# A lag of two FFN steps for w_out, in place of hand-balanced VectorE slots, in a long convolution with a maxout FFN

## The chip, the cores and the metric

The kernel runs on one core of a Trainium2 chip. The metric is the device time of one execution in microseconds (us), as the median of the runs. Engines are called PE (TensorE), DVE (VectorE), ACT (ScalarE), POOL (GpSimd) and SP (SyncE, which here only issues DMAs).

## The reference

A long convolution per channel by FFT, gated by its own input, feeds a feed-forward layer with the maximum of three products. Shapes: B = 4, S = 12544, D = 128, filter order 64, d_ff = 768; everything is float32.

```python
h_filt = (np.maximum(pos_emb @ w1, 0.0) @ w2) * np.exp(-0.01 * np.arange(S))[:, None]
u = x * v
L = 2 * S
y = np.fft.irfft(np.fft.rfft(u, n=L, axis=1) * np.fft.rfft(h_filt, n=L, axis=0)[None],
                 n=L, axis=1)[:, :S, :]
t = (x * y).reshape(B * S, D)
h = np.maximum(np.maximum(t @ moe_w1, t @ moe_w2), t @ moe_w3)
out = h @ moe_w_out
```

## The kernel before

The Fourier transforms are matmuls, done in four steps over a 128 x 98 factoring of the sequence. The filter's transform and the convolution of batch 0 come first (up to about 330 us). Then the FFN of batch b runs on PE while the convolution of batch b+1 is woven into it, for b = 0, 1, 2 (330 to about 1931 us). The FFN of the last batch runs alone at the end, in another form, with its own step order. The order of instructions on every engine is the program's order: the kernel switches the scheduler off, and each engine takes its instructions one after the other.

**FFN.** A batch has 32 tiles of 392 tokens, and a tile six steps `f`, each for 128 of the 768 hidden columns. A step is called a slot here; a batch has 192. The three-way maximum is computed as lin + max(max(a, 0), b), where a and b are products with differences of the weights and `lin` is a product folded into the output. `up` (from L689) multiplies with the first difference into `pa`, takes relu on ACT into `hid` (L694), multiplies with the second into `pb` and takes the maximum on DVE in place (L697). `down` (from L700) accumulates hid with a block of w_out into `ops`, in a tile's first step also gt with `lin`. After a tile's last step ACT copies `ops` to `ot` (L710) and POOL issues its store (L712). `pa` and `pb` rotate through three PSUM banks of the pool `hps`, `hid` through three buffers, `ops` has one bank. In slot f = 3 `t_last` makes the next tile's input: inverse-transform matmuls into `yps` and a product with x on DVE (`gt`, L684). Sums and differences of the two loaded halves (`t_sums`, `even` and `zt`) stand ahead of slot f = 1: on POOL in batch 0 and in the first half of later ones (L662, L663), on DVE in the second half (L666).

**The loop.** In each slot comes: `up` of this step, `down` of the step before it (`late`), `t_last` where due, and then the convolution's steps for this slot, from a list that `conv_steps` writes ahead.

**Convolution.** Its first part handles 32 blocks of channels (`u_` functions) and takes slots 0 to about 55 or 62. After it, 45 pairs of frequencies follow each other, spread evenly, with two or three slots between starts. Pair x starts at slot s:

- s: `g_quarter` does both matmul stages into a double bank `psq` of the pool `cps` (two such banks, shared with `yps` and the first part): the forward one of pair x and the inverse one of pair x - 3
- s+1: `g_fold` copies half of psq to `eo` on ACT (L484) and forms sum and difference on DVE into `cb` (L487, two operations of 128 x 512); half is the spectrum of pair x, half the result of x - 3, stored later by POOL (L495)
- s+2, s+3: `q_swap` exchanges real and imaginary parts on ACT into `xs` (L502 and L503 for each half of the partitions, 32 x 512 each)
- then `q_re` (L506) and `q_im` (L511) multiply with the filter's spectrum on DVE, POOL adds (L514), and `q_unfold` (L518) forms a difference and a sum of 128 x 256 on DVE for the inverse stage of three pairs later.

The planner in `conv_steps` keeps an estimate of DVE work per slot, `load`, and puts each product and each of the two unfold operations in the slot with least of it among those allowed:

```python
a = emptiest(range(s + 4, min(s + 5, last - 2) + 1), 0.7)
at(a, 0, q_re, g)
a = emptiest(range(a, min(s + 6, last - 1) + 1), 0.7)
at(a, 0, q_im, g)
for q in range(2):
    at(emptiest(range(a + 1, last + 1), 0.55), 0, q_unfold, g, q)
```

Of the kernel before, what the change touches and what calls it, by code (L numbers as in the profile page):

```python
# [9 lines left out]
FP32 = mybir.dt.float32  # L10
I32 = mybir.dt.int32
U16 = mybir.dt.uint16
ALU = mybir.AluOpType
ACTF = mybir.ActivationFunctionType
PSUM = bass.MemoryType.PSUM
P = 128
# [11 lines left out]
LATE = 3  # L28
# [61 lines left out]
def kernel(  # L90
# [15 lines left out]
    nc = tc.nc  # L106
    NG, _, _, B, NB = x.shape
    FO, S = posT.shape
    D = w2.shape[1]
    DFF = moe_w1.shape[1]  # L110
    NF = DFF // P
    NK = N1 // 2
# [37 lines left out]
    def halves_mm(out, lhsT, rhs, start, stop):  # L150


        for h in range(2):
            nc.tensor.matmul(out[64 * h:64 * h + 64], lhsT[:, 64 * h:64 * h + 64], rhs,  # L154
                             start=start, stop=stop, skip_group_check=True)
# [181 lines left out]
    us, uts, ws, hts, eos, xts, xss, abs_, pss, sqs, zss = ({} for _ in range(11))  # L337
# [157 lines left out]
        nc.gpsimd.dma_start(  # L495
            zd[b][2 * z:2 * z + 2].rearrange("k c t a f -> (k c t) a f"), zss.pop(z))

    def q_swap(g, at):
        if at == 0:
            xss[g] = cvp.tile([P, 2, 2, D], FP32, tag="xs", name="xs", bufs=3)  # L500
        xt, xs = xts[g], xss[g]
        nc.scalar.mul(xs[at:at + 32], xt[at + 32:at + 64], -1.0)  # L502
        nc.scalar.copy(xs[at + 32:at + 64], xt[at:at + 32])  # L503

    def q_re(g):
        nc.vector.tensor_tensor(out=xts[g], in0=xts[g],  # L506
# [6 lines left out]
                                op=ALU.mult)  # L513
        nc.gpsimd.tensor_tensor(out=xts[g], in0=xts[g], in1=xs[:], op=ALU.add)  # L514

    def q_unfold(g, q):
        y, ab = xts[g], xss[g]
        nc.vector.tensor_tensor(out=ab[:, q], in0=y[:, 0], in1=y[:, 1],  # L518
                                op=(ALU.subtract, ALU.add)[q])
        if q:  # L520
            abs_[g] = xss.pop(g)

    def g_second(g):
        ps = state["cv"][1].tile([P, 512], FP32, tag="cv", name="ps2")
# [47 lines left out]
    def conv_steps(b, done):  # L572


        out = []

        def at(slot, late, fn, *args):
            out.append((slot, late, len(out), fn, args))

        per_pair = 170 / (NK + LATE + 0.6 * (NU - done))
        for u in range(done, NU):
            s = (u - done) * 0.6 * per_pair + 9
            at(max(0, int(s) - 9), 0, u_load, b, u)
            at(int(s) - 6, 0, u_mul, u)
            at(int(s) - 5, 0, u_planes, u)
            at(int(s) - 4, 0, u_dma, u)
            at(int(s), 0, u_join, u)
            at(int(s + 1), 1, u_first, u)  # L590
        s0 = int((NU - done - 1) * 0.6 * per_pair + 9) + 6
        load = [(1.2 if i % NF == 3 else 0.6) + (1.4 if i % NF == 1 and b > 1 and i >= NT * NF // 2 else 0)
                for i in range(NT * NF)]
        for x in range(NK + LATE):
            load[s0 + int(x * per_pair) + 1] += 1.4

        def emptiest(among, cost):
            s = min(among, key=lambda i: load[i])
            load[s] += cost
            return s  # L600

        for x in range(NK + LATE):
            s = s0 + int(x * per_pair)
            g, z = x if x < NK else None, x - LATE if x >= LATE else None
            at(s, 1, g_quarter, g, z)
            at(s + 1, 0, g_fold, g, z)
            at(s - 4, 0, w_load, x)
            if z is not None:
                at(s + 3, 0, g_store, b, z)
            if g is None:  # L610
                continue
            if g % 2 == 0:
                at(s - 4, 0, q_load, g, min(2, NK - g))
                at(s - 1, 0, h_load, g, min(2, NK - g))
            at(s + 2, 0, q_swap, g, 0)
            at(s + 3, 0, q_swap, g, 64)
            last = s0 + int((x + LATE) * per_pair) - 1
            a = emptiest(range(s + 4, min(s + 5, last - 2) + 1), 0.7)
            at(a, 0, q_re, g)
            a = emptiest(range(a, min(s + 6, last - 1) + 1), 0.7)  # L620
            at(a, 0, q_im, g)
            for q in range(2):
                at(emptiest(range(a + 1, last + 1), 0.55), 0, q_unfold, g, q)
        slots = {}
        for s, _, _, fn, args in sorted(out, key=lambda r: r[:3]):
            slots.setdefault(s, []).append((fn, args))
        return slots
# [3 lines left out]
    NT = P // 4  # L631
    zts, xTs, gs, pos_, obs = ({} for _ in range(5))

    def t_load(b, i):
        zt = hp.tile([N1, 2, 512], FP32, tag="zt", name="zt", bufs=2)
        for c in range(2):
            if b == 0:
                nc.sync.dma_start(
                    zt[NK * c:NK * c + NK],
                    zd[b].rearrange("(g a) c t f -> g a c t f", a=2)[  # L640
                        :, :, c, 2 * i:2 * i + 2, :].rearrange("g a t f -> g a (t f)"))
                continue
            q, j = divmod(i, NT // 2)
            for a in range(2):
                nc.sync.dma_start(
                    zt[NK * c:NK * c + NK, a].rearrange("g (t f) -> g t f", t=2),
                    zd[b].rearrange("(g a) c t q f -> g a c t q f", a=2)[
                        :, a, c ^ (a & q), 2 * j:2 * j + 2, q, :])
        zts[b, i] = zt[:, 0], zt[:, 1]
        if i % 2:  # L650
            return
        xT = hp.tile([D, 2, 4, NB], FP32, tag="xT", name="xT", bufs=2)
        for c in range(GC):
            nc.sync.dma_start(xT[c * NG:(c + 1) * NG].rearrange("d i p n -> d (i p) n"),
                              x[:, 4 * i:4 * i + 8, c, b, :])
        xTs[b, i], xTs[b, i + 1] = xT[:, 0], xT[:, 1]

    def t_sums(i, eng=nc.gpsimd):
        z0, z1 = zts[i]
        even = hp.tile([N1, 512], FP32, tag="even", name="even", bufs=2)  # L660
        if i[0] == 0 or i[1] < NT // 2:
            eng.tensor_tensor(out=even[:], in0=z0, in1=z1, op=ALU.add)  # L662
            eng.tensor_tensor(out=z1, in0=z0, in1=z1, op=ALU.subtract)  # L663
        else:
            for out, op in ((even[:], ALU.add), (z1, ALU.subtract)):
                nc.vector.scalar_tensor_tensor(out=out, in0=z1, scalar=sign_t[:, 0:1], in1=z0,  # L666
                                               op0=ALU.mult, op1=op)
        zts[i] = even[:], z1
# [31 lines left out]
    def down(i, f, h):  # L700
        if f == 0:
            pos_[i] = ops.tile([D, 512], FP32, tag="ops", name="ops")
            halves_mm(pos_[i][:, 0:N], lin[:], gs[i][:].rearrange("d p n -> d (p n)"), True,
                      False)
        halves_mm(pos_[i][:, 0:N], wo_sb[:, f, :], h[:], False, f == NF - 1)
        if f < NF - 1:
            return
        gs.pop(i)
        o = op_.tile([D, 4, NB], FP32, tag="o", name="ot")
        nc.scalar.copy(o[:].rearrange("d p n -> d (p n)"), pos_.pop(i)[:, 0:N])  # L710
        dst = outT.rearrange("d (p b n) -> d p b n", b=B, n=NB)[:, 4 * i[1]:4 * i[1] + 4, i[0], :]
        nc.gpsimd.dma_start(dst, o[:])  # L712
# [160 lines left out]
    for u in range(0, NU, 2):  # L873
        t = uts.pop(u)
        for v in range(2):
            if u + 4 < NU:
                u_mul(u + 4 + v)
            at = 4 * (u + v)
# [11 lines left out]
    for i in (1, 2):  # L890
        nc.vector.tensor_tensor(out=w_sb[i][:], in0=w_sb[i][:], in1=w_sb[0][:],
                                op=ALU.subtract)
# [3 lines left out]
    cvp = pro.enter_context(tc.tile_pool(name="cvp0", bufs=3))  # L896
# [123 lines left out]
    cvp = conv.enter_context(tc.tile_pool(name="cvp", bufs=3))  # L1020
# [5 lines left out]

    tiles = [(b, i) for b in range(B) for i in range(NT)]
    LAST = (B - 1) * NT
    late = None
    for n, (b, i) in enumerate(tiles[:LAST]):  # L1030
        if i == 0:
            beside = {}
            beside = conv_steps(b + 1, EARLY if b == 0 else 0)
        if n == 0:
            t_load(*tiles[0])
            t_load(*tiles[1])
            t_sums(tiles[0], nc.vector)
            t_last(tiles[0])
        for f in range(NF):

            if i < NT - 2:
                if f == 0:
                    t_load(*tiles[n + 2])
            elif i == NT - 1 and f < 2 and n + 1 + f < len(tiles):
                t_load(*tiles[n + 1 + f])
            turn_ = i == NT - 1
            if f == (3 if turn_ else 1):
                t_sums(tiles[n + 1], nc.vector if turn_ else nc.gpsimd)
            if f == 4 and n + 1 == LAST:
                t_sums(tiles[n + 2], nc.vector)  # L1050
            h = up((b, i), f)
            if late is not None:
                down(*late)
            late = ((b, i), f, h)
            if f == (4 if turn_ else 3):
                t_last(tiles[n + 1])
            if f == 5 and n + 1 == LAST:
                t_last(tiles[n + 2])
            s = i * NF + f
            run(beside.pop(s, ()))  # L1060
            if s == NT * NF - 1:
                assert not beside, sorted(beside)
    first = up((B - 1, 0), 0)
    down(*late)
    conv.close()


# [20 lines left out]
    step, b = 0, B - 1  # L1088
    for i in range(0, NT, 2):
        h = {}  # L1090
# [63 lines left out]
```

## Time and profile before

| | |
|---|---|
| median of 3 runs | 2353.33 us (2351.71 to 2353.9) |
| profiled execution | 2353.33 us, its span 2351.5 us |
| mean granted PE clock | 0.995 |
| PE busy 330 to 842, 842 to 1387, 1387 to 1931 us | 509.2, 536.7, 533.7 us |
| DVE busy in the same | 340.6, 377.4, 379.3 us |
| ACT busy in the same | 273.8, 288.1, 286.9 us |
| relu, L694 | 768 of 499 ns |
| maximum, L697 | 768 of 558 ns |
| exchange, L502 and L503 | 270 of 628 ns, 270 of 616 ns |
| fold, L487 (128 x 512) | 252 of 683 ns |
| products, L506 and L511 | 135 of 689 ns, 135 of 738 ns |
| unfold, L518 | 270 of 468 ns |

The durations are means of one profiled execution and include whatever slowed an instruction down while it ran; the timeline shows each one by itself. A wait in the profile is the idle time of an engine before an instruction, put down to what released it last.

### The profile page before, as it was taken

To read this page: it belongs to the slowest core of one execution; us is meant where nothing else is said; L and a number is where in the kernel's file an instruction comes from. 1 tells how busy PE (TensorE), PEld (TensorE's weight loads), DVE (VectorE), ACT (ScalarE), POOL (GpSimd) and SP (SyncE) were. 2 spreads that over 40 slices of the span, in tenths; PEclk is the share of its full clock that TensorE was granted. 3 is DMA by queue.
4 is the path that set the end of the run, shared out by engine and by line. 5 is a ranking of instruction groups with operands and counts; after the bars stand their busy time and mean duration, and the time that the engine had idled before them with its cause. 6 is when DMAs were issued, how large, how long until landed. Compare 5 with 4: busy or idle time off the path is not lost.

```text
span 2351.5 us, 67998 instructions
## 1 busy us (share of the span) xinstructions
PE 2300.1 (98%) x27853; PEld 1373.9 (58%) x27853; DVE 1528.8 (65%) x2798; ACT 1172.7 (50%) x2124; POOL 976.0 (42%) x1153
## 2 busy tenths in 40 slices
PE   8999989999999999999999999999999999999998
PEld 7889866655545546654454446655454546666665
DVE  5668857756777747757787747757777755444443
ACT  2678844456665624446666624446666632222222
POOL 1045424334444434434333324434333326666666
PEclk9999999999999999999999999999999999999999
DMA  7869969979898869969899849969899922222221
GB/s 163 195 192 267 292 154 187 165 173 230 225 240 218 206 126 190 187 144 239 226 236 240 221 114 190 187 139 241 229 231 242 229 81 70 56 54 66 68 54 22
DMA packets 473145, 410.92 MB, mean 175 GB/s; under 512 B 328004, under 2 KB 374231, under 8 KB 472834
## 3 DMA queue, kind: packets, MB, share of 16 engines
q1 hardware_dynamic: 433504, 317.61, 60.9%
q0 software_dynamic: 26400, 75.72, 11.1%
q10 hardware_dynamic: 12930, 13.25, 1.8%
q8 instruction: 219, 3.59, 0.7%
q14 instruction: 92, 0.75, 0.1%
HBM read 262.77 MB, written 84.67 MB: 148 GB/s over the span
## 4 chain that ended last, share of the span: by engine, by line
PE 87%; DMA 5%; DVE 2%; issue 2%; ACT 2%; SPq 0%; POOL 0%; ACTq 0%; POOLq 0%; DVEq 0%
PE pa L154 20%; PE pb L154 19%; PE ops L154 16%; PE ops L757 6%; PE ps L408 5%; PE yps L154 5%; PE psq L462 3%; PE ps L163 3%; PE ps L154 3%; PE psq L472 2%; PE gps L926 1%; PE sps L944 1%; DMA zt<-zd 1%; DMA wt<-wq_const 1%; PE pm L323 1%
## 5 line engine op out<-in xcount | busy, mean ns | idle before, releaser
L694 ACT ACTIVATE hid<-pa 128x392 f32<-128x392 f32 x768 | 383.4, 499 | 683.0 <-PE pa L154 657.3
L697 DVE TENSOR_TENSOR hid<-hid,pb 128x392 f32<-128x392 f32 x768 | 428.7, 558 | 425.6 <-PE pb L154 332.5
L154 PE MATMUL pa<-gt,w_sb 128*64 128x392 f32 x3072 | 648.3, 499 | 0.8 <-DVE gt L684 0.8
L154 PE MATMUL pb<-gt,w_sb 128*64 128x392 f32 x3072 | 638.9, 493 | 3.6 <-ACT hid L694 3.6
L154 PE MATMUL ops<-hid,wo_sb 128*64 128x392 f32 x2304 | 478.9, 493 | 15.6 <-DVE hid L697 15.6
L154 PEld LDWEIGHTS pb<-gt,w_sb 128*64 128x64 f32 x3072 | 223.3, 137 | 288.2 <-issue 271.0
L514 POOL TENSOR_TENSOR cb<-cb,xs 128x512 f32<-128x512 f32 x135 | 174.9, 1296 | 444.5 <-DVE xs L511 155.0
L154 PEld LDWEIGHTS ops<-hid,wo_sb 128*64 128x64 f32 x2304 | 165.7, 137 | 232.6 <-issue 168.4
L154 PEld LDWEIGHTS pa<-gt,w_sb 128*64 128x64 f32 x3072 | 196.1, 137 | 137.8 <-issue 93.2
L712 POOL DMA_DIRECT2D out_dram<-ot x96 | 74.6, 777 | 422.4 <-ACT ot L710 285.8
L502 ACT ACTIVATE xs<-cb 32x512 f32<-32x512 f32 x270 | 169.5, 628 | 111.5 <-DVE cb L487 107.3
L487 DVE TENSOR_TENSOR cb<-psq,eo 128x512 f32<-128x512 f32 (+1 forms) x288 | 175.1, 649 | 72.5 <-ACT eo L484 72.5
L419 DVE TENSOR_TENSOR spec<-ps,high 128x360 f32<-128x360 f32 (+1 forms) x204 | 142.0, 738 | 114.3 <-ACT high L417 113.8
L503 ACT COPY xs<-cb 32x512 f32<-32x512 f32 x270 | 166.3, 616 | 3.1
L417 ACT COPY high<-ps 128x360 f32<-128x360 f32 (+1 forms) x102 | 77.3, 762 | 170.2 <-PE ps L408 112.7
L408 PEld LDWEIGHTS ps<-f1q,uT 98*64 98x64 f32 x3072 | 132.2, 137 | 34.6 <-issue 32.4
L154 PEld LDWEIGHTS yps<-f4p,even 90*64 90x64 f32 x2048 | 116.3, 138 | 41.0 <-issue 36.4
L408 PE MATMUL ps<-f1q,uT 98*64 98x90 f32 x3072 | 136.6, 241 | 3.1 <-DVE spec L419 2.6
L684 DVE TENSOR_TENSOR gt<-yps,xT 128x392 f32<-128x392 f32 x128 | 72.5, 567 | 97.7 <-PE yps L154 55.6
L154 PE MATMUL yps<-f4p,even 90*64 90x49 f32 x2048 | 125.6, 221 | 3.3 <-DMA f4p<-f4p_const 3.3
L154 PE MATMUL yps<-f4p,zt 90*64 90x49 f32 x2048 | 127.4, 223 | 0.0
L518 DVE TENSOR_TENSOR xs<-cb 128x256 f32<-128x256 f32 x270 | 115.9, 468 | 3.6 <-POOL cb L514 3.1
(130 smaller groups left out, 3343.0 us busy)
## 6 DMA issues: line engine op xcount, KB each, us to landing
ht<-hd SPq DMA_DIRECT2D x264, 256.0 KB, 5.9
wt<-wq_const SPq DMA_DIRECT2D x144, 256.0 KB, 6.7
zd<-cb POOLq DMA_DIRECT2D x135, 256.0 KB, 6.1
zt<-zd SPq DMA_DIRECT2D x384, 90.0 KB, 3.2
sq<-spec SPq DMA_DIRECT2D x264, 128.0 KB, 7.2
ut<-in_xr_dram SPq DMA_DIRECT2D x128, 196.0 KB, 4.1
ut<-in_vr_dram SPq DMA_DIRECT2D x128, 196.0 KB, 4.3
xT<-in_x_dram SPq DMA_DIRECT2D x256, 98.0 KB, 4.0
```

The costliest lines, as they stand in the source:

```text
L154: nc.tensor.matmul(out[64 * h:64 * h + 64], lhsT[:, 64 * h:64 * h + 64], rhs, start=start, stop=stop, skip_group_check=True)
L408: nc.tensor.matmul(ps[64 * c:64 * c + 64, 256 * i + h * N1:256 * i + (h + 1) * N1], t[:, 2 * ((at + i) % 8) + h].rearrange("n r t -> n (r ...
L417: nc.scalar.copy(high, v[:, 0])
L419: nc.vector.tensor_tensor(out=spec[:, :, a, at:at + n], in0=v[:, 1], in1=high, op=op)
L487: nc.vector.tensor_tensor(out=cb[:, a, lo:hi], in0=ps[:, lo:hi], in1=eo[:, lo:hi], op=op)
L502: nc.scalar.mul(xs[at:at + 32], xt[at + 32:at + 64], -1.0)
L503: nc.scalar.copy(xs[at + 32:at + 64], xt[at:at + 32])
L514: nc.gpsimd.tensor_tensor(out=xts[g], in0=xts[g], in1=xs[:], op=ALU.add)
L518: nc.vector.tensor_tensor(out=ab[:, q], in0=y[:, 0], in1=y[:, 1], op=(ALU.subtract, ALU.add)[q])
L694: nc.scalar.activation(h[:], pa[:, 0:N], Relu)
L697: nc.vector.tensor_tensor(out=h[:], in0=h[:], in1=pb[:, 0:N], op=ALU.max)
L757: nc.tensor.matmul(ps[64 * c:64 * c + 64, 0:H2], w, rhs[:, H2 * c:H2 * c + H2], start=start, stop=True, skip_group_check=True)
```

## The change

Two things change. The product with w_out is held back by two steps in place of one: `late` becomes a list, and `down` takes its oldest entry once it has more than two; after the loop both that are left are done. And the placing by load is gone from `conv_steps`, with `load` and `emptiest`: the four operations of the exchange are one call at s+2, the products come at s+3 and s+4, and both unfold operations in one call at s+6.

```diff
+    def q_swap(g):
+        xt = xts[g]
+        xs = cvp.tile([P, 2, 2, D], FP32, tag="xs", name="xs", bufs=3)
+        for at in (0, 64):
+            nc.scalar.mul(xs[at:at + 32], xt[at + 32:at + 64], -1.0)
+            nc.scalar.copy(xs[at + 32:at + 64], xt[at:at + 32])
+        xss[g] = xs
...
+    def q_unfold(g):
+        y, ab = xts.pop(g), xss.pop(g)
+        for q, op in enumerate((ALU.subtract, ALU.add)):
+            nc.vector.tensor_tensor(out=ab[:, q], in0=y[:, 0], in1=y[:, 1], op=op)
+        abs_[g] = ab
...
-            at(s + 2, 0, q_swap, g, 0)
-            at(s + 3, 0, q_swap, g, 64)
-            last = s0 + int((x + LATE) * per_pair) - 1
-            a = emptiest(range(s + 4, min(s + 5, last - 2) + 1), 0.7)
-            at(a, 0, q_re, g)
-            a = emptiest(range(a, min(s + 6, last - 1) + 1), 0.7)
-            at(a, 0, q_im, g)
-            for q in range(2):
-                at(emptiest(range(a + 1, last + 1), 0.55), 0, q_unfold, g, q)
+            at(s + 2, 0, q_swap, g)
+            at(s + 3, 0, q_re, g)
+            at(s + 4, 0, q_im, g)
+            at(s + 6, 0, q_unfold, g)
...
-    late = None
+    late = []
...
             h = up((b, i), f)
-            if late is not None:
-                down(*late)
-            late = ((b, i), f, h)
+            late.append(((b, i), f, h))
+            if len(late) > 2:
+                down(*late.pop(0))
...
     first = up((B - 1, 0), 0)
-    down(*late)
+    for l in late:
+        down(*l)
     conv.close()
```

More of the change, by code (lines that the diff above doesn't have):

```diff
@@ L496, in g_store @@
             zd[b][2 * z:2 * z + 2].rearrange("k c t a f -> (k c t) a f"), zss.pop(z))
[L498 to L503, printed above, removed]
+    def q_swap(g):
[5 more added lines that the diff above has]
+        xss[g] = xs
     def q_re(g):
@@ L514, in q_im @@
         nc.gpsimd.tensor_tensor(out=xts[g], in0=xts[g], in1=xs[:], op=ALU.add)
[L516 to L521, printed above, removed]
+    def q_unfold(g):
[3 more added lines that the diff above has]
+        abs_[g] = ab
     def g_second(g):
@@ L591, in conv_steps @@
         s0 = int((NU - done - 1) * 0.6 * per_pair + 9) + 6
[L592 to L600, printed above, removed]
         for x in range(NK + LATE):
```

## The prediction

> **What bounds the kernel now.** I began with the page: TensorE (PE) is busy for 98% of a span of 2351.5 us at a clock of 0.995, so what another engine costs must show as PE waiting.
>
> ```profile
> PE 2300.1 (98%) x27853; PEld 1373.9 (58%) x27853; DVE 1528.8 (65%) x2798; ACT 1172.7 (50%) x2124; POOL 976.0 (42%) x1153
> ```
>
> The view of waits therefore comes next; its columns are total us, times, longest us.
>
> ```profile
> PE ops L154 <- DVE hid L697: 15.6, 13, 1.8
> PE pb L154 <- ACT hid L694: 3.6, 1, 3.6
> ACT xs L502 <- DVE cb L487: 107.3, 107, 3.0
> DVE cb L487 <- ACT eo L484: 72.5, 62, 2.4
> ```
>
> Of 51 us of PE idle time only 15.6 us wait for a maximum of VectorE (DVE), and these 13 waits are what a later `down` can save: five of 0.32 and eight of 1.76 us. The 3.6 us is one wait at the step into the last batch. The last two rows matter more: ScalarE (ACT) and DVE wait for each other along each pair, in the order fold, exchange, evacuation, fold.
>
> I then read the timeline, all engines, around one of the 1.76 us waits. Columns: start, duration, engine, line, operation.
>
> ```profile
> 1242.91 1.28 DVE L487 TENSOR_TENSOR cb<-psq,eo 128x512 f32<-128x512 f32 x2
> ...
> 1244.28 0.63 ACT L502 ACTIVATE xs<-cb 32x512 f32<-32x512 f32 x1 [0.76 <-DVE cb L487]
> ...
> 1247.88 0.49 ACT L710 COPY ot<-ops 128x392 f32<-128x392 f32 x1 [0.82 <-PE ops L154]
> ...
> 1248.39 0.63 ACT L502 ACTIVATE xs<-cb 32x512 f32<-32x512 f32 x1
> ...
> 1249.03 0.61 ACT L503 COPY xs<-cb 32x512 f32<-32x512 f32 x1
> ...
> 1249.67 0.59 ACT L484 COPY eo<-psq 128x512 f32<-128x512 f32 x1
> 1250.15 0.50 ACT L694 ACTIVATE hid<-pa 128x392 f32<-128x392 f32 x1
> 1250.29 1.29 DVE L487 TENSOR_TENSOR cb<-psq,eo 128x512 f32<-128x512 f32 x2 [2.10 <-ACT eo L484]
> ```
>
> The reader is to see two things. The exchange starts 0.09 us after the fold ends (1244.19), and every later ACT step stands behind it. And in the slot where `ot` is copied too, the second half of the exchange makes `eo` late, DVE idles 2.10 us before the fold, its next maximum ends at 1253.48, and PE waits.
>
> **The slots on PE.** From the same timeline, matmul start to matmul start: pa, pb and one w_out product take 0.66 each, so a slot takes 1.97 us; a pair's stage (psq) adds 1.13, and once in six slots `yps` adds 0.92 and `lin` 0.66 (1.58 per tile).
>
> **What the later `down` is worth.** A maximum must now be ready when the next slot's pb ends, 1.97 us (plus the slot's own convolution matmuls) after its own pb. With a lag of two, `down` asks for it a slot later, but the three `hps` banks ask sooner: pa of slot k+2 takes the bank of pb of slot k. That is 0.66 us plus the next slot's convolution matmuls more than now. The wait above gets 0.66 + 1.13 = 1.79 us for its 1.76: all 15.6 us go. What the lag does not move is the other half of the rotation: pb of slot k+1 takes the bank of pa of slot k, so it waits for the relu of slot k on ACT as before.
>
> What moves along at nothing: `hid` has three buffers, and the `down` that frees one stands before the next pa on PE; `ot` is copied and its store issued on POOL one slot later, behind the sums of that slot; `ops` is free again after the same distance. If one of these showed it would be at tile ends, 96 times; the nearest row is the ot copy, 0.49 us (47 us in all, both ways). I take none of it, since ot stands no closer to its next user. SP's queue gets nothing moved. POOL's pair sum (1.27 us) moves with the second product, and its result is needed two slots (over 3.9 us) later.
>
> **What the fixed places cost.** The change makes the four exchange operations one block in slot s+2 and fixes the first product at s+3, the second at s+4, both unfold operations at s+6, where before they went to the emptiest slots. Pairs follow each other after 2 or 3 slots. Working out which slot gets what, the slot of a fold (s+1) now nearly always holds, ahead of the fold, the unfold of an earlier pair and one product.
>
> Durations, uncontended, from the timeline: exchange operations 0.63 and 0.62, relu 0.50, maximum 0.55, unfold pair 0.75, product 0.68, fold 1.28; handovers 0.02 to 0.09.
>
> Now follow a pair. Its fold starts the exchange, 2.51 us; behind it on ACT stands the relu of slot s+3; behind that the maximum on DVE; behind that unfold and product; then the next pair's fold. That is a loop:
>
> - two slots apart: 0.09 + 2.51 + 0.02 + 0.50 + 0.03 + 0.55 + 0.02 + 0.75 + 0.02 + 0.68 + 0.02 + 1.28 = 6.47 us, against 2 x 1.97 + 1.13 = 5.07 on PE;
> - three slots apart: one maximum and one product more, 7.74 us, against 7.04 on PE.
>
> In the kernel before, the two-slot loop runs through half the exchange, relu, the other half, eo, fold: 0.09 + 1.25 + 0.02 + 0.50 + 0.02 + 1.25 + 0.02 + 0.59 + 0.03 + 1.28 = 5.05, just under PE's 5.07, which is why it waits only where ot joins in. In the new one the loop is longer than PE's work, and PE waits at pb for the relu.
>
> The sum by batch (pairs 0 to 44 of each: 15 two-slot and 30 three-slot steps in the first convolution, 22 and 23 in the two others). On the loop's DVE part fall also the `gt` product (0.57) in 10, 12 and 12 tiles and, in the second half of the two later ones, the sums of zt (1.65) in 9 tiles each; elsewhere they lie beside the exchange.
>
> - first: 15 x 6.47 + 30 x 7.74 + 10 x 0.57 = 335.0; PE 120 x 1.97 + 45 x 1.13 + 20 x 1.58 = 318.9; difference 16.1
> - each other: 22 x 6.47 + 23 x 7.74 + 12 x 0.57 + 9 x 1.65 = 342.1; PE 113 x 1.97 + 45 x 1.13 + 19 x 1.58 = 303.5; difference 38.6
>
> Together 93.3 us. Off go 12: in each batch the first three folds are half as wide (0.45 less each), two loops have no unfold yet (0.75 each) and the first 1.1 us is slack. Off go the 15.6. On come some 5 for restarts: a matmul after a wait takes 0.88 and not 0.83, perhaps 90 times. Net +70.
>
> Ends. With the groups' mean durations, which hold collisions with POOL (fold 1.37, unfold 0.94, products 0.69 and 0.74, exchange 2.55, sums 1.81), the loops are 6.82 and 8.15 and the same sum gives 148 in place of 93: +125. With `gt` and the zt sums all hidden (19 and 30 us off) it gives +21. I stay with the uncontended end, because behind the second product, while POOL adds, DVE runs the fold or nothing.
>
> The collision is seen in the row of an unfold pair beside POOL's sums, 2.17 us where it takes 0.75 alone. The Trainium skill, "SBUF — State Buffer", section "SBUF: two separate sides", says that of a GpSimd operation and a VectorE operation with two SBUF inputs the one that comes second waits for the other's whole length; the pair's extra 1.42 us fits this, and an estimate by that page, blocking once in every pair, would lift the sum by at most 135 x 1.27 = 171 us.
>
> ACT is busy half the time and yet holds PE up here. The Trainium skill, "Perfetto Trace Analysis", section "Optimizing Scalar/DVE Operations", says that where such an engine is not saturated but causes gaps elsewhere, breaking work up may let it finish sooner; by that rule joining the two halves speaks against this change, and by occupancy alone it would cost nothing (2338, the first rival).
>
> **Rivals.**
> Faster: the relus are never late, and the lag's 15.6 us is all that shows: 2353 - 16 = 2338. It decides at one point: PE waits at pb when the fold ends later than 7.70 - 3.12 = 4.58 us after its slot's start (7.70 is three slots, a psq and a pa; 3.12 the exchange and relu). A fold alone in a free slot ends at 3.45; up to 1.1 us of other work ahead of it costs nothing. For it: in the timeline above it ended at 4.07 with an unfold ahead, and ACT held PE up once only. Against it: the new lists put 1.43 us ahead of most folds.
>
> No change: the three-slot steps, with the tile's extra 0.79 us, give the 1.1 us of slack back each time, so a two-slot step's shortage (1.40, less 0.53 of tile matmuls) is swallowed, and only the 18 zt sums show, 0.5 to 1.65 us each: +9 to +30 less 15.6, 2347 to 2368. Against it: 7.74 plus `gt` is no shorter than 7.04 + 0.79, so little is given back.
>
> **How the numbers follow.** The profiled run took 2353.33 us, which is the median of the runs; its span is 2351.5. So the forecast is 2353 + 70 = 2423, with its own range from +21 (2374) to +125 (2478). Chances: the loop 0.78, beyond its upper end 0.03, no change 0.08, faster 0.11. The range of 2362 to 2478 takes in the loop's cases and the upper part of "no change". A measurement here tells 0.2% (4.7 us) from no change: faster by more 0.12, within 0.04, slower by more 0.84.
>
> **What would show it.** Right: the wait of ops for hid (15.6 us) gone or below 3; a new row, pb waiting for ACT hid, of 60 to 110 us in 70 to 120 waits of about 1 us; nearly all in the pair stage, the two later batches worse than the first; DVE waiting longer for ACT hid than the 89.6 us now. Wrong: a pb row under 10 us, or PE waiting mainly at pa for DVE, which would make VectorE the bound and not the exchange.

## The result

The changed kernel takes 2375.54 us (median of 4 runs, 2374.38 to 2377.9) against 2352.52 us: a ratio of 1.0102, with a 95% interval of 1.0085 to 1.0120. That is slower by 23 us where +70 was forecast: the sign and the mechanism held, the size did not, by a factor of three. The profiled run took 2377.9 us, its span 2376.1. Helper lines after the planner have moved: the relu is L679 (was L694), the maximum L682 (L697), the unfold L520 (L518), the products L507 and L512.

The busy shares on the page look nearly like those before; DVE and ACT are a little less busy. The group of the w_out product has lost its idle time (last column), the fold no longer waits for `eo`, and pb has a wait that it did not have.

```profile
PE 2312.2 (97%) x27853; PEld 1372.2 (58%) x27853; DVE 1489.2 (63%) x2798; ACT 1165.4 (49%) x2124; POOL 968.7 (41%) x1153
...
L154 PE MATMUL pb<-gt,w_sb 128*64 128x392 f32 x3072 | 644.9, 497 | 33.3 <-ACT hid L679 33.3
...
L154 PE MATMUL ops<-hid,wo_sb 128*64 128x392 f32 x2304 | 478.5, 492 | 0.0
...
L487 DVE TENSOR_TENSOR cb<-psq,eo 128x512 f32<-128x512 f32 (+1 forms) x288 | 174.6, 647 | 2.5 <-ACT eo L484 2.5
```

The view of waits (total us, times, longest) shows what took their place. The maximum waits for the late relu 244.2 us where it was 89.6, the exchange for the fold 196.2 where it was 107.3.

```profile
DVE hid L682 <- ACT hid L679: 244.2, 114, 2.7
...
ACT xs L502 <- DVE cb L487: 196.2, 121, 2.8
...
PE pb L154 <- ACT hid L679: 33.3, 53, 3.7
```

The timeline of one turn of the loop, from the start of one pair's exchange to the next one's, two slots apart:

```profile
1187.31 0.63 ACT L502 ACTIVATE xs<-cb 32x512 f32<-32x512 f32 x1 [1.96 <-DVE cb L487]
...
1189.22 0.61 ACT L503 COPY xs<-cb 32x512 f32<-32x512 f32 x1
...
1189.86 0.50 ACT L679 ACTIVATE hid<-pa 128x392 f32<-128x392 f32 x1
...
1190.39 0.56 DVE L682 TENSOR_TENSOR hid<-hid,pb 128x392 f32<-128x392 f32 x1 [2.70 <-ACT hid L679]
...
1190.41 0.88 PE L154 MATMUL pb<-gt,w_sb 128*64 128x392 f32 x4 [0.46 <-ACT hid L679]
...
1190.87 0.75 DVE L520 TENSOR_TENSOR xs<-cb 128x256 f32<-128x256 f32 x2
...
1191.54 0.68 DVE L507 TENSOR_TENSOR cb<-cb,ht 128x512 f32<-128x512 f32 x1
1192.14 1.28 DVE L487 TENSOR_TENSOR cb<-psq,eo 128x512 f32<-128x512 f32 x2
...
1193.51 0.63 ACT L502 ACTIVATE xs<-cb 32x512 f32<-32x512 f32 x1 [2.28 <-DVE cb L487]
```

Each step is the one named in the prediction, in its order, and PE waits at pb. But the turn takes 1193.51 - 1187.31 = 6.20 us, not 6.47. The reason is in the start times of DVE: the maximum starts at 1190.39 and lasts 0.56, yet the unfold starts at 1190.87, 0.48 later. The unfold pair takes 0.67 from start to start, the product 0.60, and the two fold operations 1.20 to the next maximum. A duration in the profile reaches some 0.08 us into the next instruction.

Added over the trace, by how much later pb starts after pa than the usual 0.66 us, the waits in the pair stage delay PE by 8.5, 13.7 and 13.5 us in the three batches: 35.7 us. In slots 6 and 7 of each batch another 1.5 us is lost (4.6 in all). The lag took away 17.8 us of delay at ops. The balance, 35.7 + 4.6 - 17.8 = 22.5 us, is close to the 23.0 between the medians.

### The profile page after: what moved, and what is told of

The parts are those of the page before. It is cut to its first block, busy times and chain, and to the rows that moved or that the text cites. A ratio compares the mean times of both kernels' runs of the same rounds, so it can differ in the third digit from the quotient of the medians.

```text
span 2376.1 us, 68062 instructions
## 1 busy us (share of the span) xinstructions
PE 2312.2 (97%) x27853; PEld 1372.2 (58%) x27853; DVE 1489.2 (63%) x2798; ACT 1165.4 (49%) x2124; POOL 968.7 (41%) x1153
## 4 chain that ended last, share of the span: by engine, by line
PE 78%; ACT 8%; DMA 5%; DVE 4%; issue 3%; ACTq 0%; POOL 0%; SPq 0%; DVEq 0%; POOLq 0%
PE pb L154 19%; PE pa L154 19%; PE ops L154 16%; PE ops L742 6%; PE ps L408 5%; PE yps L154 5%; PE ps L163 3%; PE psq L462 2%; ACT xs L503 2%; ACT xs L502 2%; DMA hd<-ht 2%; DVE cb L487 2%; PE psq L472 2%; ACT hid L679 1%; ACT ht L934 1%
## 5 line engine op out<-in xcount | busy, mean ns | idle before, releaser
L682 DVE TENSOR_TENSOR hid<-hid,pb 128x392 f32<-128x392 f32 x768 | 428.0, 557 | 556.4 <-PE pb L154 305.4
L679 ACT ACTIVATE hid<-pa 128x392 f32<-128x392 f32 x768 | 381.7, 500 | 639.5 <-PE pa L154 620.8
L154 PE MATMUL pb<-gt,w_sb 128*64 128x392 f32 x3072 | 644.9, 497 | 33.3 <-ACT hid L679 33.3
L154 PEld LDWEIGHTS pb<-gt,w_sb 128*64 128x64 f32 x3072 | 217.3, 137 | 338.9 <-issue 236.9
L502 ACT ACTIVATE xs<-cb 32x512 f32<-32x512 f32 x270 | 169.4, 628 | 199.5 <-DVE cb L487 196.2
L697 POOL DMA_DIRECT2D out_dram<-ot x96 | 75.1, 783 | 323.1 <-ACT ot L695 285.5
L408 PEld LDWEIGHTS ps<-f1q,uT 98*64 98x64 f32 x3072 | 133.3, 137 | 35.7 <-issue 31.4
L377 POOL COPY planes<-ut 128x784 uint16<-128x784 uint16 x90 | 75.9, 843 | 135.6 <-DVE ut L356 135.4
```

Source lines behind the costliest of these rows:

```text
L377: nc.gpsimd.tensor_copy(pl_[:, :, :, 0:NB], a[:].bitcast(U16).rearrange("p s (n h) -> p h s n", h=2))
L408: nc.tensor.matmul(ps[64 * c:64 * c + 64, 256 * i + h * N1:256 * i + (h + 1) * N1], t[:, 2 * ((at + i) % 8) + h].rearrange("n r t -> n (r ...
L679: nc.scalar.activation(h[:], pa[:, 0:N], Relu)
L682: nc.vector.tensor_tensor(out=h[:], in0=h[:], in1=pb[:, 0:N], op=ALU.max)
```

## The experiments

Two explanations of the slowdown were set against each other: the loop of fold, exchange, relu and maximum, made too long by the joined exchange together with the fixed places; and, as rivals, the lag itself, or one of the other parts by itself. The median of the kernel before differs by a few us from one set of runs to the next (2348.75 to 2355.37), so ratios within a set are compared.

| exchange, places | order in slot | lag | ratio to before | 95% interval |
|---|---|---|---|---|
| joined, fixed (the change) | as listed | 2 | 1.0102 | 1.0085 to 1.0120 |
| halves, by load | as listed | 2 | 0.9967 | 0.9956 to 0.9978 |
| joined, fixed | as listed | 1 | 1.0151 | 1.0136 to 1.0166 |
| joined, by load | as listed | 1 | 0.9988 | 0.9978 to 0.9998 |
| joined, fixed | fold first | 2 | 0.9926 | 0.9911 to 0.9941 |
| halves, fixed | as listed | 2 | 0.9940 | 0.9927 to 0.9952 |
| halves, fixed | fold first | 2 | 0.9940 | 0.9926 to 0.9954 |
| halves, by load | fold first | 2 | 0.9963 | 0.9951 to 0.9976 |
| joined, fixed | fold first | 1 | 1.0117 | 1.0103 to 1.0131 |

**The lag alone.** The kernel before with the change's second half only.

```diff
-            if late is not None:
-                down(*late)
-            late = ((b, i), f, h)
+            late.append(((b, i), f, h))
+            if len(late) > 2:
+                down(*late.pop(0))
```

> The lag of two alone, with the exchange in halves and the DVE work placed by load as before. Theory (the joined exchange and the fixed places make the loop fold, exchange, relu, maximum, fold longer than PE's work; the lag itself only takes waits away): the 13 waits of ops for hid go (15.6 us idle, about 18 with the restarts), the 0.76 us waits of pb in slots 6 and 7 of each batch seen in the changed kernel (about 4.6 us in all) come with the lag, so 2337 to 2342 us, and pb waits for ACT hid under 9 us including the 3.6 at the last batch. Rival (the lag itself is the cost: PE runs a step further ahead and so meets the relu at pb): pb waits of 30 us as in the changed kernel and 2360 to 2376.

Measured: 2345.91 us against 2353.23. From PE's waits, 330 to 1960 us:

```profile
PE pb L154 <- ACT hid L694: 7.3, 7, 3.7
PE psq L462 <- DMA wt<-wq_const: 4.3, 4, 2.5
```

The ops row is gone, and pb shows only the last batch's wait and six short ones in slots 6 and 7. So the lag does not cost what the change lost; it brings 0.3%. It fell short of the 2337 to 2342 expected by 4 us, and the profile has about that in matmuls of psq that wait for a load. Why the loads are late in this kernel and not in those with fixed places was not settled.

**The rest of the change, lag of one.** The changed kernel with `down` held back by one step, as before.

```diff
-            if len(late) > 2:
+            if len(late) > 1:
```

> The joined exchange and the fixed places alone, with the lag of one as before. Theory: the same pb waits of about 30 us, and besides, PE waits at ops for hid, because in two-slot pairs the maximum behind the fold ends about 3.6 us after the late relu and a lag of one asks for it after 2.7: 2385 to 2415 us. Rival (the lag is the cost): near 2352, since the lag is as before.

Measured: 2389.18 us, as the theory had it, but with the waits elsewhere:

```profile
PE ops L154 <- DVE hid L682: 29.9, 28, 2.0
PE pb L154 <- ACT hid L679: 4.1, 10, 0.5
```

With a lag of one PE meets the late maximum at ops before it meets the late relu at pb. The expectation had added the two; they are the same lateness, met at one place or the other.

**The joined exchange alone.** The kernel before, both halves in slot s+2.

```diff
             at(s + 2, 0, q_swap, g, 0)
-            at(s + 3, 0, q_swap, g, 64)
+            at(s + 2, 0, q_swap, g, 64)
```

> Only the exchange joined into one block in slot s+2; products and unfold placed by load and the lag of one as before. Theory: from the start-to-start times of the changed kernel's timeline the two-slot loop is 2.55 + 0.53 + 0.48 + 0.67 (at most one unfold pair or product ahead of the fold) + 1.37 = 5.6 us against 5.07 on PE and 0.53 of the tile's own matmuls, so hardly longer: 2348 to 2362 us. Rival (the joined block on ACT is the whole cost, the places on DVE cost nothing): 2375 to 2390, pb waits of 25 us or more.

Measured: 2350.70 us, no slower than before.

```profile
PE ops L154 <- DVE hid L697: 3.3, 8, 0.6
```

The 15.6 us wait of before has shrunk to 3.3: with the second half gone from the next slot, it no longer stands ahead of `eo` where `ot` is copied. In the turn shown in the prediction the 2.10 us that DVE idled ahead of the fold are 0.70 here, and the wait of 1.76 us is 0.35: 1.4 us less in both. At the lag of one, and with the places by load, joining costs nothing.

**Fold first.** The changed kernel; the fold stands ahead of the other DVE work of its slot.

```diff
-            at(s + 1, 0, g_fold, g, z)
+            at(s + 1, -1, g_fold, g, z)
```

> The changed kernel with one difference: in its slot the fold stands ahead of the unfold and the products on DVE. Theory: the loop loses 0.6 to 1.3 us a pair, the two-slot one becomes 2.55 + 0.53 + 0.48 + 1.37 = 4.93 us against 5.07, and the pb waits of the pair stage go; the 4.6 us in slots 6 and 7 stay: 2337 to 2346 us. Rival (the block of four on ACT by itself, or the lag, is the cost): 2368 to 2378 as the changed kernel.

Measured: 2336.64 us, 0.4 us under the expected range and 1.7% below the changed kernel by the ratios, with the same instructions on every engine.

```profile
PE pb L154 <- ACT hid L679: 7.3, 7, 3.8
```

Where the loop is tightest, two-slot exchanges now follow each other after 4.93 or 4.94 us (16 turns), where the sum said 4.93; in two turns at the start of a pair stage, with folds half as wide, it is 4.57. The pair stage's pb waits are gone. This is the experiment that shows the loop: nothing was taken away; unfold and products (1.27 us in the turn above) were moved from ahead of the fold to behind it, beside the exchange.

**The exchange in halves, fixed places.** The changed kernel with `q_swap` of before.

```diff
-            at(s + 2, 0, q_swap, g)
+            at(s + 2, 0, q_swap, g, 0)
+            at(s + 3, 0, q_swap, g, 64)
```

> The changed kernel with the exchange in halves again (slots s+2 and s+3), fixed places and the lag of two kept. Theory: the two-slot loop goes through half the exchange, relu, the other half and then product and fold: 1.27 + 0.53 + 1.27 + 0.03 + 0.60 + 1.37 = 5.07 us, PE's own 5.07; the 36 us of pb waits in the pair stage go nearly all, so neither the join nor the places cost much alone: 2336 to 2350 us. Rival (the fixed places on DVE are the cost, whatever the exchange): 2365 to 2378.

Measured: 2335.30 us against 2348.75, 0.7 us under the expected range. The pb row is down to 7.3 us here too:

```profile
PE pb L154 <- ACT hid L679: 7.3, 7, 3.7
```

So the fixed places, without the join, cost nothing at the lag of two. Join and places are harmless one at a time (the join was tried alone at the lag of one) and together delay PE by the 35.7 us of the pair stage: the loop is at PE's pace with one of them and beyond it with both.

**Fold first in the two other settings.** The same one-line edit in the kernel before with the lag, and in the kernel with halves and fixed places.

> The kernel before (exchange in halves, DVE work placed by load) with the lag of two, and in its slot the fold ahead of other DVE work. Theory: with the lag alone the loop was already shorter than PE's work, so the order inside the slot has nothing left to save but chance waits for loads: 2334 to 2346 us, pb waits for ACT hid at 7 us. Rival (fold-first is worth something of its own beyond the loop): clearly below the fixed places with the fold first, 2325 to 2332.

> Fixed places, lag of two, exchange in halves and the fold first in its slot: the loop is 1.27 + 0.53 + 0.48 + 1.37 = 3.65 us, far under 5.07. Theory: nothing more to gain than with the joined exchange and the fold first, because a loop under PE's work costs nothing: 2333 to 2341 us. Rival (ACT's backlog still costs something in that kernel): 2320 to 2330.

Measured: 2340.26 and 2335.25 us, both inside what the theory expected, and at the ratios of the kernels without the edit (0.9963 beside 0.9967, 0.9940 beside 0.9940). Where the loop is already shorter than PE's work, making it shorter brings nothing.

**Fold first, lag of one.** The changed kernel with the edits of fold first and of the lag of one together.

> Fixed places, joined exchange and the fold first in its slot, with the lag of one: what the lag is worth once the loop is short. Theory: pb waits stay near the 3.7 us of the last batch, and ops waits for hid where unfold and product behind the fold make the next maximum late by up to 0.7 us: 2340 to 2356 us. Rival (the lag brings nothing): 2334 to 2339, like the lag of two.

Measured: 2375.42 us, 19 us beyond the upper end of what the theory expected.

```profile
PE ops L154 <- DVE hid L682: 35.5, 29, 3.1
```

The relu is in time now and the pb row holds only the last batch's 3.3 us, but behind the fold come unfold and product: from one maximum to the next DVE needs 0.48 + 1.20 + 0.67 + 0.60 = 2.95 us, and a lag of one allows 1.97 where no convolution matmul lies between. I had looked at one place only. This turn by itself gives short waits, 0.3 us in 11 of the 29. In the 17 long ones more stands between the two maxima: in 12, of 1.3 to 1.6 us, the two sums of zt, and in 5 of the first batch, of 2.5 to 3.1 us, an unfold pair that takes 2.6 to 3.1 us beside POOL's sums. With this order of DVE work the lag is worth 1.0117 - 0.9926 = 1.9%, not the 0.3% that it brings to the kernel before.

**A dose on the loop.** The changed kernel with the second unfold operation done twice.

```diff
-        for q, op in enumerate((ALU.subtract, ALU.add)):
+        for q, op in enumerate((ALU.subtract, ALU.add, ALU.add)):
+            q = min(q, 1)
```

> The changed kernel with the second unfold operation of each pair done twice (same operands, same result): one more DVE instruction of about 0.34 us, start to start, ahead of nearly every fold, on a DVE that is 63% busy. Theory: the loop sets the pace in the pair stage, so most of 135 x 0.34 = 46 us shows: two-slot loops of 6.54 and three-slot loops of 7.6 us between exchange starts in place of 6.20 and 7.27, and 2400 to 2422 us. Rival (the pb waits come from single collisions, not from a loop at its limit): DVE's idle time swallows it, 2374 to 2385 us.

Measured: 2423.65 us, ratio 1.0286 (1.0262 to 1.0309), that is 1.8% or 43 us above the changed kernel by the ratios, and 1.7 us over the expected range.

```profile
PE pb L154 <- ACT hid L680: 66.9, 93, 1.8
```

The turns became 6.66 and 7.74 us, 0.46 longer and not 0.34. Most of 135 x 0.46 = 62 us reached the end, although DVE stands idle for a third of the span. That is what a loop at its limit does; single collisions would have left most of it in the idle time.

## Why the prediction was right and wrong

**Right: where the waits go.** The 15.6 us at ops went to 0.0, the lag left pb tied to the relu, and PE now waits there. The pair stage carries it, the two later batches more than the first (13.7 and 13.5 against 8.5 us). DVE's wait for the relu rose as said. The row itself came to 33.3 us in 53 waits, where 60 to 110 us in 70 to 120 waits had been named as the sign. The rival "faster" is in kind what the lag does alone, without the places (2345.91 us). The rival "no change" fell as a forecast, but its argument had a part in it: a three-slot turn of 7.27 us is shorter than PE's 7.04 + 0.79, so slack is given back there, and PE waits in 46 slots of the pair stage and not once in each of the 135 turns.

**Wrong: the length of the loop.** The step that failed is the list of durations laid end to end: 6.47 and 7.74 us. The turns between exchange starts in the changed kernel are 6.20 and 7.27 us where nothing else joins in (34 of 57 two-slot and 18 of 75 three-slot turns). The lists counted 0.08 us too much, and a handover of 0.02 besides, for each DVE operation that another follows at once. This is 0.27 us in 59 two-slot and 0.47 us in 76 three-slot steps, 52 us of the 93: an error of 4 to 6% in a loop that is compared with something almost as long. With the turns as measured the sum is, for the first batch, 15 x 6.20 + 30 x 7.27 + 10 x 0.5 - 318.9 = -2.8 us, and for each other 22 x 6.20 + 23 x 7.27 + 12 x 0.5 + 9 x 1.5 - 303.5 = 19.6 us: 36 in all, where 35.7 was measured. (The `gt` product and the sums of zt take 0.5 and 1.5 from start to start, not 0.57 and 1.65.) With this in place of 93 and its other terms as they stood, the prediction would have read 36 - 12 - 15.6 + 5 = +14 us against the measured 23. The agreement is closer than the sum deserves: the first batch shows 8.5 us and not -2.8, because where PE is the slower one for a while the loop gains no more than its small slack. That loss and the 12 us taken off for the start about cancel; the first pb waits of the pair stage do come only 16 or 17 slots after it begins.

Both loops could have been had from the timeline of before. There too the product at 1204.30 lasts 0.68 and is followed at 1204.90. The Trainium skill, "Perfetto Trace Analysis", section "Optimizing Scalar/DVE Operations", says that the profiled latency holds a part that overlaps with the next instruction; the 0.08 us seen here agrees in kind. It gives about 60 ns of access overhead for VectorE on SBUF and about 125 on PSUM, and the profiled latency as about twice that; an estimate by that page would put the overlap at 0.06 or 0.125 us. Here it is 0.08 both for the product, which reads SBUF, and for the maximum, which reads pb from PSUM; both write SBUF, so no operation here shows a difference between the two.

**Wrong: the upper end.** The group means, with collisions in them, were the further from the truth. The choice of the uncontended durations was right in direction and did not go far enough. That the lower end, +21, lies next to the measured 23 is luck: it took `gt` and the sums of zt as hidden, and what was too long was the turn. The argument that joining goes against breaking work up was loose too: the four exchange operations stay four, 628 and 616 ns long as before, and only what stands between them changed.

**Overlooked: the sums of zt.** The 1.76 us wait of before has a second part, which stands between the late fold and the maximum:

```profile
1251.49 0.74 DVE L666 SCALAR_TENSOR_TENSOR even<-zt,sign 90x512 f32<-90x512 f32 x1
1252.27 0.75 DVE L666 SCALAR_TENSOR_TENSOR zt<-zt,sign 90x512 f32<-90x512 f32 x1
1252.93 0.55 DVE L697 TENSOR_TENSOR hid<-hid,pb 128x392 f32<-128x392 f32 x1
```

All eight waits of 1.76 us have these two sums there, 1.44 us from start to start; the five of 0.32 us, in the first batch, where POOL does them, have not. In the changed kernel the two later batches lose some 1.4 us each up to slot 90 and some 12 from slot 91 on, where DVE does the sums; in the sum above they are 13.5 of the 19.6 us. Nor is DVE always at the fold or idle while POOL adds: eight times the second of the sums takes 1.64 us beside POOL's pair sum, where it takes 0.75 alone. The fold first takes the waits away with the sums in place; how much would stay without them in the order as listed was not tried.

**Missing: slots 6 and 7.** I had taken nothing for what moves along with the lag. Every kernel with a lag of two loses 1.5 us per batch here, none with a lag of one does. In the changed kernel's timeline:

```profile
876.76 0.83 PE L154 MATMUL pa<-gt,w_sb 128*64 128x392 f32 x4
...
877.63 0.50 ACT L679 ACTIVATE hid<-pa 128x392 f32<-128x392 f32 x1 [1.48 <-PE pa L154]
...
878.18 0.88 PE L154 MATMUL pb<-gt,w_sb 128*64 128x392 f32 x4 [0.60 <-ACT hid L679]
```

pb waits for the relu of its own slot, though ACT was idle before it. That would fit pb having been given the bank that pa of the same slot has just filled, so that the three banks do not rotate there as I had read them; no run shows which bank it got, and the cause was not tested. It is 4.6 us of the 23.

**Restarts.** The 5 us for them, 0.05 in each of some 90, were too few. The wait that the profile shows at 1190.41 is 0.46 us, while pb started 1.29 us after pa and not 0.66, a delay of 0.63: the row understates its cost by about 0.2 us. The 46 waits of the pair stage show 26.0 us and delay PE by over 35.

**The version that beats both.** Fixed places with the lag of two, and either the fold first (0.9926) or the exchange in halves (0.9940): 13 to 17 us below the kernel before. Their intervals overlap, so no choice between the two is shown.

## What to carry to other kernels

Two engines that are busy for half and two thirds of the time can hold up a third one that is busy for 97%, if each waits for the other once per turn: add up the turn, not the shares, and compare it with the bottleneck's work per turn. Take the steps of such a turn from start to start in the timeline, since durations overlap; where the turn is within a few per cent of the other side, that overlap decides the size. And in the slot of an instruction that another engine waits for, put it ahead of the work that nobody waits for yet: here one line of order was worth 1.7%.

## What the runs showed of the hardware

- A DVE instruction's duration in the profile exceeds its start-to-start time by about 0.08 us when the next follows at once: 0.56 and 0.48 for the maximum, 0.68 and 0.60 for the product, 0.75 and 0.67 for the unfold pair. On ACT the exchange, which reads SBUF, shows no such overlap: 0.63 and 0.62 long, 0.64 and 0.63 apart. The relu, which reads PSUM, does: 0.50 long, with `eo` 0.39 after it.
- The repeated unfold operation added 0.46 us to a turn, more than the 0.34 between two different ones. It writes where the one before it has just written; whether that is the reason was not tried.
- One lag of the consumer on PE was worth 0.5% with the fold as listed and 1.9% with the fold first (both with the joined exchange and fixed places), and 0.3% in the kernel before.
- Two sums of 90 x 512 on DVE took 0.75 us each alone, and the second 1.64 where POOL's sum of 128 x 512 ran beside it (1195.19 us in the changed kernel).
